# Moving a quarter of the convolution's products behind step 184 and re-pacing the convolution in a fused attention and long-convolution kernel

## The chip, the cores and the metric

The kernel runs on one core of one Trainium2 chip. The metric is the time of one execution on the device in microseconds; lower is better. A core has five engines that each run their own instruction list in order: PE (TensorE, matrix products), ACT (ScalarE, exponentials here), DVE (VectorE), POOL (GpSimd) and SP (SyncE, here only a queue that issues DMAs). They meet through semaphores.

## The reference

Two independent blocks share the launch, and their outputs are written side by side. Block A is multi-head attention with 32 heads of width 16 over 2048 tokens. Block B is a long convolution over 2048 steps for 512 channels, written with FFTs: `kv` is a 4-tap short convolution of `k` times `v`, then every channel is convolved with its own filter of length 2048, and gated by `q`.

```python
# A: x (1,2048,512), wqkv (512,1536), wo (512,512), H = 32, Dh = 16
qkv = (x @ wqkv) -> q, k, v per head
p   = softmax(q k^T * Dh**-0.5)          # 32 heads x 2048 x 2048
a   = (p v) reshaped to (1,2048,512) @ wo
# B: q, k, v (1,2048,512), shift_k (512,4), ssm_k (512,2048), ssm_D (512)
k_shift = sum_t k_pad[:, t:t+S, :] * shift_k[:, 3-t]
kv = k_shift * v
y  = irfft(rfft(kv padded to 4096) * rfft(ssm_k padded to 4096))[:, :2048]
b  = q * (y + kv * ssm_D)
out = concatenate([a, b], axis=-1)
```

## The kernel before, in words

**Attention.** The scores are cut into 2048 blocks of 128 keys by 512 queries. They are handled in 741 *steps*; a step makes the scores of two or three blocks (L539, four row groups of PE at a time), and one ACTIVATE (L550) takes the exponential of all of them from PSUM. From step 56 on, one block of a three-block step can go to DVE instead, which makes its exponential with a polynomial in five instructions: one to leave PSUM (L586), three Horner steps (L593) and a last one (L598). Two steps later the block is multiplied with the values (L632). A finished group is turned on DVE, divided by its sums, and turned back into the tile OTN (L718), whose eight slots feed the output product (L749).

**Convolution.** It is a Toeplitz product on PE. The reversed filters are written to a scratch in HBM (`kz_scratch`), and for each channel a 128 x 2048 Toeplitz tile is read back with overlapping rows: `load_wr` issues four such loads of 512 KB on SP for a *column group* `qd` of four channels. There are 128 column groups and a ring of three in SBUF (WR). `conv_lags` (L804) multiplies one group in 16 *lags* of four small products each, in column-tiled form, so there are 2048 lags in all, and they go through PSUM bank 7. The products `kv` themselves are made on PE too: a unit `("kv", c, i)` multiplies 128 channels of transposed keys (KTR) with diagonal tap matrices DG (which lie in OTN slots 4 to 7), and DVE multiplies by the values on the way out (`evac_unit`, L393). Column group `qd` needs the products of its quarter, `qd // 32`.

**The plan.** All instruction lists are written out in advance by a Python planner with its own clock: each engine has a planned time (`Eng.op`), each DMA a planned landing (`dma`, a single chain at DMA_KB kilobytes per us). In step T it emits the scores, the value products, then `emit_bg(T)`. That first lets `unit_step` place half a unit (projections of queries, keys and values, kv products, output products, and transposes of the finished convolution, "turn") if it fits before the end of the current exponential, or is forced by its due step; then it fills what is left (`room`, up to a margin) with conv lags. Until step 184 (N_EARLY) the units come from an ordered list `early`, and one PSUM bank is kept free for them throughout; after it they come from `next_unit`, by due step, in 25 slots of five steps each from step 190 on, 21 steps apart.

The lags are limited by a pace and by the planned landing of the loads:

```python
left_us = max(1.14 * (NT - END - T), 1.0)
st["lags"] = min(st["lags"] + min(PACE * st["left"] / left_us, RATE) * (pe.t - st["t"]), CAP)
left = min(LAGS, int(st["lags"]), int((room(T) - 0.06) / 0.055))
while left > 0 and ... at(h_wr[st["qd"]]) + WAIT <= pe.t:
```

and a load on the chip waits for the conv that frees its ring slot. In the kernel before, keys are loaded transposed (`load_kt`) in two slabs of 256 channels: into QN for quarters 0 and 1 and into the second half of QT for quarters 2 and 3. Both are loaded early, after the filters have been reversed on DVE (`kz_turn`). The values for quarter 2 lie in VS2, those for quarter 3 in OUTA. The weights WK (keys) and WV (values, later replaced by the output weights WO) are the halves of WKV; WK is last read by the key projection `("k", 3, 3)`.

Of the kernel before, what the change touches and what calls it, by code (L numbers as in the profile page):

```python
# [11 lines left out]
S = 2048  # L12
D = 512
H = 32
DH = 16
QB = 512
NQB = S // QB
KT = S // 128
NG = 8
# [4 lines left out]
C = 512  # L24
# [11 lines left out]
BGB = 7  # L36
N_EARLY = 184
LAGS = 6
PACE = 1.2
KEYS0 = 256  # L40
END = 16

# [20 lines left out]
GAP = 7  # L63
TAIL_GAP = 4
AHEAD = 4
KZ_LATE = 4.0
KEEP = 4
BACKLOG = 3.9
MARGIN = 0.35
SPARE = 0.1  # L70
DMA_KB = 400.0
WINDOW = 3.4
BUSY = 0.75
FILL_GAP = 0.25
RATE = 3.4
CAP = 10.0
WAIT = 1.0
LATE = 0.6
V512 = (0.60, 0.726)

# [54 lines left out]
def bass_concat_heads__mha_block__ssm_conv_h3__prompt_kernel(  # L135
# [24 lines left out]
    def sb(name, shape, dt=BF16):  # L160
# [14 lines left out]
    WQ = sb("WQ", [128, 4, D])  # L175
    PAT = sb("PAT", [1, 2, 128])
    MASK = sb("MASK", [128, 2], FP32)
    WKV = sb("WKV", [128, 2, 4, D])
    OTN = sb("OTN", [128, R_O, QB])
    DT = sb("DT", [128, QB], FP32)  # L180
    DTN = sb("DTN", [128, 2, QB])
# [8 lines left out]
    EH = sb("EH", [128, R_EH, QB], FP32)  # L190
    ZW = sb("ZW", [128, 32])
    JNK = sb("JNK", [128, 2], FP32)
    WK = WKV[:, 0, :, :]
    WV = WKV[:, 1, :, :]
    WO = WV
    VST = [x.rearrange("p (t d) -> p t d", t=NB)
           for x in (WR[:, 8, :], WR[:, 9, :], VS2[:, :], OUTA[:, :, :].rearrange("p r d -> p (r d)"))]
    KZS = WRF[:, 0:4 * LKZ].rearrange("p (c m) -> p c m", c=4)
    DSS = WRF[:, 4 * LKZ:4 * LKZ + 4].rearrange("p (c m) -> p c m", m=1)
    KTR = [QNF[:, 0:2 * LKR].rearrange("p (c s) -> p c s", c=2),  # L200
           QTF[:, NG * QB:NG * QB + 2 * LKR].rearrange("p (c s) -> p c s", c=2)]
# [54 lines left out]

    d_w = [DmaSem(sem(f"d_w{i}")) for i in range(5)]
    d_x = [DmaSem(sem(f"d_x{i}")) for i in range(4)]
    d_kv = [DmaSem(sem(f"d_kv{i}")) for i in range(6)]
# [28 lines left out]
    h_vn, h_kt, h_kt0 = [], {}, {}  # L288
    for c in range(4):
        src = bass.AP(tensor=v2.tensor, offset=v2[128 * (NB - 1), 128 * c].offset, ap=[[D, 128], [-128 * D, NB], [1, 128]])  # L290
        h_vn.append(dma(sp, d_kv[2 + c], VST[c], src, kb=1024))

    def load_kt(i, dep):
        h_kt[i] = dma(sp, d_kv[i], KTR[i][:, :, LEFT:LEFT + S], k2[:, 256 * i:256 * i + 256], [dep], transpose=True, kb=1024)
        h_kt0[i] = pool.op(lambda e: e.memset(KTR[i][:, :, 0:LEFT], 0.0), [dep])


# [19 lines left out]
    def unit_deps(u):  # L317
        if u[0] == "q":
            return h_x[u[1]] + [h_wq[min(u[2], 1)]]
        if u[0] == "k":  # L320
            return h_x[u[2]] + [h_wk[min(u[1], 1)]]
        if u[0] == "kv":
            return [h_kt[u[1] // 2], h_dg[0]]
        return h_x[u[1] // 4] + [h_wv]

    def pe_unit(u, bank, dcs=(0, 1, 2, 3)):
        kind = u[0]
        deps = [bank_free[bank]]
        mm_us, mm_run = 0.215, 0.213
        if kind == "q":  # L330
            _, qb, o = u
            deps += h_x[qb] + [h_wq[min(o, 1)]]

            def mm(e, dc):
                return e.matmul(PS[:, bank, :], lhsT=WQ[:, dc, o * 128:(o + 1) * 128], rhs=xT[:, dc, qb * 512:(qb + 1) * 512],  # L335
                                start=(dc == 0), stop=(dc == 3))
        elif kind == "k":
            _, o, sc = u
            c0 = KEYS0 if (o, sc) == (0, 0) else 0
            deps += h_x[sc] + [h_wk[min(o, 1)]]  # L340
            mm_us, mm_run = (512 - c0) / 512 * 0.215, (512 - c0) / 512 * 0.213

            def mm(e, dc):
                return e.matmul(PS[:, bank, c0:512], lhsT=WK[:, dc, o * 128:(o + 1) * 128],  # L344
                                rhs=xT[:, dc, sc * 512 + c0:(sc + 1) * 512], start=(dc == 0), stop=(dc == 3))
        elif kind == "kv":
            _, c, i = u
            deps += [h_kt[c // 2], h_kt0[c // 2], h_dg[0]]
            mm_us, mm_run = 0.27, 0.21

            def mm(e, b):
                ins = None
                for m in range(4):
                    c0 = LEFT + 128 * (4 * i + 3 - b) - m
                    ins = e.matmul(PS[:, bank, 128 * b:128 * b + 128], lhsT=KTR[c // 2][:, c % 2, c0:c0 + 128], rhs=DG[:, c, m, :],
                                   start=(m == 0), stop=(m == 3))
                return ins
        else:
            _, kt = u
            deps += h_x[kt // 4] + [h_wv]  # L360

            def mm(e, dc):
                return e.matmul(PS[:, bank, :], lhsT=xT[:, dc, kt * 128:(kt + 1) * 128], rhs=WV[:, dc, :],  # L363
                                start=(dc == 0), stop=(dc == 3))

        def fn(e):
            ins = None
            for dc in dcs:
                ins = mm(e, dc)
            return ins  # L370
        return pe.op(fn, deps, us=(0.105 + mm_us * len(dcs), 0.235 + mm_us * len(dcs)),
                     run=mm_run * len(dcs))

    def evac_unit(u, bank, h):
        kind = u[0]
        if kind == "q":
            _, qb, o = u
            for par in range(2):
                hh = h_q[(qb, 2 * o + par)] = urgent(
                    lambda e, par=par: e.tensor_scalar(QT[:, qb % 2, 2 * o + par, :], PS[:, bank, :], MASK[:, par:par + 1], None, ALU.mult),  # L380
                    [h, h_mask] + ([h_kzt[0], h_kvm[0]] if qb == 1 else []), us=V512)
        elif kind == "k":
            _, o, sc = u
            c0 = KEYS0 if (o, sc) == (0, 0) else 0
            hh = urgent(lambda e: e.tensor_copy(KTo[:, o, sc * 512 + c0:(sc + 1) * 512], PS[:, bank, c0:512]), [h],
                        us=(0.335, 0.46) if c0 else V512)
            h_k[(o, sc)] = hh
        elif kind == "kv":
            _, c, i = u
            dst = KV[:, 32 * c:32 * c + 32, NB - 4 - 4 * i:NB - 4 * i, :]  # L390
            val = VST[c][:, NB - 4 - 4 * i:NB - 4 * i, :].rearrange("p b (k c) -> p k b c", c=4)
            src = PS[:, bank, :].rearrange("p (b k c) -> p k b c", b=4, c=4)
            h_kvc[c] = hh = urgent(lambda e: e.tensor_tensor(dst, src, val, ALU.mult), [h, h_vn[c]], us=V512)  # L393
            kv_n[c] += 1
            if sum(kv_n[0:2]) == 8 and c < 2:
                load_qn(0, [h])
                wr_free.append((2, hh))
                load_wr()
            if sum(kv_n) == 16:
                h_kvm[0] = h  # L400
        else:
            _, kt = u
            dst = VAF[:, kt, 0:H * VW].rearrange("p (h e) -> p h e", e=VW)[:, :, 0:DH]
            src = PS[:, bank, :].rearrange("p (h e) -> p h e", h=H)
            hh = urgent(lambda e: e.tensor_copy(dst, src), [h, h_vaf1], us=V512)  # L405
            h_v[kt] = hh
        bank_free[bank] = hh

    h_kvc = [None] * 4
    kv_n = [0] * 4  # L410
    h_kvm = [None]
    wr_free = []
    wr_next = [0]
    h_kzw = [None]
# [274 lines left out]
    def finish_group(n, h, T):  # L689
# [21 lines left out]
        def turn_back(i0, i1, us):  # L711
# [3 lines left out]
                deps += [h_op[((p - R_O) // 4, t)] for t in range(4)]  # L715
            if p == 4:
                deps.append(h_kvm[0])
            h_otn[(p, i1)] = h_otn[p] = dve.op(lambda e: e.transpose(out=OTN[:, p % R_O, sl], in_=dtn[:, sl]), deps, us=us)  # L718

        def may_turn():  # L720
            return 2 * p in h_mul and 2 * p + 1 in h_mul and (p < R_O or all(((p - R_O) // 4, t) in h_op for t in range(4)))
        u_r, u_m, u_t = (0.155, 0.28), (0.334, 0.46), (0.6, 0.75)
        if last:
            recip(u_r)
# [39 lines left out]
    def op_out_end(qb, t, bank, h):  # L764
# [3 lines left out]
        else:  # L768
            hh = dve.op(lambda e: e.tensor_copy(dst, PS[:, bank, :]), [h])
        r0 = qb * QB + t * 128  # L770
        dma(act if t % 2 else sp, d_outE, out2[r0:r0 + 128, 0:D], dst, [hh])


    h_wr, h_qn = {}, {}
# [49 lines left out]
    def conv_turn(b, bank):  # L824
# [34 lines left out]
    state = {"qd": 0, "lag": 0, "turn": False, "q": 0, "op": 0, "started": False, "lags": 0.0,  # L859
             "left": C // 4 * NB, "t": 0.0}  # L860
# [10 lines left out]
    def next_unit(T):  # L871
# [158 lines left out]
    for T in range(NT + 3):  # L1030
# [5 lines left out]
        emit_bg(T)  # L1036
        warm_up(T)
        advance(pe.t)
    assert state["qd"] == C // 4 and not state["turn"] and state["q"] == len(later_q) and state["op"] == len(later_op), state
    assert not early_dve and not flow and not acts and not dves  # L1040


# [62 lines left out]
```

## Time and profile before

| | |
|---|---|
| median of 6 runs | 863.8 us (859.77 to 874.42) |
| the profiled execution | 859.77 us |
| its span, first to last instruction | 858.0 us |
| mean granted TensorE clock | 0.992 |
| ACT busy | 836.8 us, 98% |
| DVE busy | 782.8 us, 91% |
| PE busy (pipelined, an upper figure) | 743.3 us, 87% |
| HBM read and written | 276.83 MB, 6.42 MB |
| Toeplitz loads | 512 of 512 KB, median 8.0 us from issue to landing |
| score blocks exponentiated on DVE | 213 of 2048 |

Every time of a view below is in microseconds from the start of the span. In the view of groups and waits, "A <- B: 7.8, 20, 1.1" says that A waited for B for 7.8 us in all, 20 times, at most 1.1 us. L numbers are lines of the kernel; SPq is SP's DMA queue. In a table of windows each engine's busy time is followed by its instruction count; then come the granted PE clock (1.00 is full speed), the mean busy share of the 16 DMA engines and GB/s.

Today's places of the moved work: the sixteen kv evacuations (L393) run from 80.7 to 184.1 us, those of quarter 2 from 151.5 to 163.8 and those of quarter 3 from 169.4 to 184.1. Step 184 begins near 204 us.

### The profile page before, as it was taken

The numbers are of one execution on the slowest core, as the hardware profiler recorded it, in microseconds if no ns is written. First come the engines' busy times: TensorE is split into PE (matmuls) and PEld (weight loads), VectorE is DVE, ScalarE is ACT, GpSimd is POOL, SyncE is SP. The second block draws the span as 40 slices with busy tenths as digits, with TensorE's granted clock in tenths as the row PEclk, the third lists the DMA queues.
The fourth block names the chain that finished last, engine by engine and source line by source line (L and its number), as shares of the span: only waits on it lengthen the run. The fifth ranks groups of instructions, "written<-read, shape, count | busy, mean of one in ns | idle before, by whom it ended". The sixth has DMA issues, their size and how long they took to land.

```text
span 858.0 us, 29424 instructions
## 1 busy us (share of the span) xinstructions
PE 743.3 (87%) x13184; PEld 302.2 (35%) x13184; DVE 782.8 (91%) x1330; ACT 836.8 (98%) x746; POOL 17.3 (2%) x33
## 2 busy tenths in 40 slices
PE   7988999998888888888888888888888888888877
PEld 2223343443333333333333333333333333333332
DVE  2328999999999999999999999999999999999994
ACT  6999999999999999999999999999999999999997
POOL 2000000000000000000000000000000000000000
PEclk9999999999999999999999999999999999999999
DMA  9970069879999999999999999999999999999942
GB/s 269 258 239 1 1 207 341 279 233 328 407 407 410 361 401 396 399 407 398 387 396 373 355 392 388 407 379 394 407 408 366 408 399 410 406 394 408 407 189 74
DMA packets 104813, 289.36 MB, mean 337 GB/s; under 512 B 35184, under 2 KB 37232, under 8 KB 104304
## 3 DMA queue, kind: packets, MB, share of 16 engines
q1 hardware_dynamic: 99424, 279.35, 86.2%
q0 software_dynamic: 1808, 6.29, 2.2%
q8 instruction: 104, 1.70, 0.8%
q10 hardware_dynamic: 3456, 1.84, 0.8%
q14 instruction: 21, 0.17, 0.0%
HBM read 276.83 MB, written 6.42 MB: 330 GB/s over the span
## 4 chain that ended last, share of the span: by engine, by line
ACT 61%; DMA 16%; DVE 11%; PE 9%; SPq 2%; issue 1%; ACTq 0%
ACT PT L550 61%; DMA WR<-kz_scratch 15%; DVE EH L593 5%; PE PS L539 3%; PE PS L804 2%; DVE PTD L598 2%; SPq L223 2%; PE PS L632 2%; DVE FX L586 2%; DMA xT<-in_A_x_dram 1%; PE PS L363 1%; DVE QT L380 1%; DVE DT L696 1%; PE PS L749 0%; DVE YB L819 0%
## 5 line engine op out<-in xcount | busy, mean ns | idle before, releaser
L550 ACT ACTIVATE PT<-PS 128x1536 bf16<-128x1536 f32 (+1 forms) x741 | 833.8, 1351 | 8.7 <-PE PS L539 7.8
L539 PE MATMUL PS<-QT,KTo 32*128 32x512 bf16 x2048 | 303.2, 387 | 85.5 <-ACT PT L550 68.4
L593 DVE SCALAR_TENSOR_TENSOR EH<-EH,FX 128x512 f32<-128x512 f32 x426 | 281.9, 678 | 0.0
L804 PE MATMUL PS<-WR,KV 128*5 128x128 bf16 (+15 forms) x8192 | 223.5, 221 | 14.6 <-DMA WR<-kz_scratch 12.6
L632 PE MATMUL PS<-PT,VAF 128*32 128x512 bf16 x1835 | 201.6, 392 | 3.7 <-DVE DT L696 2.5
L804 PEld LDWEIGHTS PS<-WR,KV 128*2 128x2 bf16 (+15 forms) x8192 | 149.6, 88 | 100.6 <-issue 40.4
L539 PEld LDWEIGHTS PS<-QT,KTo 32*128 32x128 bf16 x2048 | 72.9, 91 | 263.5 <-ACT PT L550 228.1
L586 DVE TENSOR_SCALAR FX<-PS 128x512 f32<-128x512 f32 x213 | 145.2, 682 | 5.8 <-PE PS L539 5.4
L598 DVE SCALAR_TENSOR_TENSOR PTD<-EH,FX 128x512 uint16<-128x512 f32 x213 | 143.5, 676 | 0.0
L593 DVE SCALAR_TENSOR_TENSOR EH<-FX 128x512 f32<-128x512 uint16 x213 | 143.2, 680 | 0.0
L632 PEld LDWEIGHTS PS<-PT,VAF 128*32 128x32 bf16 x1835 | 48.5, 93 | 119.0 <-issue 105.8
L1012 PE MATMUL PS<-IDN,ZW 128*32 128x512 bf16 (+3 forms) x229 | 72.4, 316 | 0.0
L632 PE MATMUL PS<-PTD,VAF 128*32 128x512 bf16 x213 | 60.3, 385 | 0.0
L405 DVE CAST VAF<-PS 128x512 bf16<-128x512 f32 x16 | 11.1, 692 | 30.2 <-PE PS L363 30.2
L696 DVE STREAM_TRANSPOSE DT<-PS 128x512 f32<-128x512 f32 x31 | 22.1, 711 | 12.8 <-PE PS L632 12.2
L1012 PEld LDWEIGHTS PS<-IDN,ZW 128*32 128x32 bf16 x229 | 22.2, 97 | 11.6 <-issue 10.3
L819 DVE CAST YB<-PS 128x512 bf16<-128x512 f32 x32 | 21.8, 680 | 2.3 <-PE PS L804 2.3
L380 DVE TENSOR_SCALAR QT<-PS,MASK 128x512 bf16<-128x512 f32 x30 | 21.0, 742 | 3.0 <-PE PS L335 2.8
L363 PE MATMUL PS<-WKV,xT 128*128 128x512 bf16 x64 | 18.9, 384 | 1.8 <-DVE VAF L405 1.2
L749 PE MATMUL PS<-WKV,OTN 128*128 128x512 bf16 x64 | 19.7, 385 | 0.3 <-DVE OTN L718 0.3
L344 PE MATMUL PS<-xT,WKV 128*128 128x512 bf16 (+1 forms) x64 | 18.3, 377 | 1.1 <-DVE QT L380 0.5
L335 PE MATMUL PS<-xT,WQ 128*128 128x512 bf16 x60 | 18.2, 384 | 0.1
(66 smaller groups left out, 195.5 us busy)
## 6 DMA issues: line engine op xcount, KB each, us to landing
WR<-kz_scratch SPq DMA_DIRECT2D x512, 512.0 KB, 8.0
kz_scratch<-WR SPq DMA_DIRECT2D x1, 2176.0 KB, 8.5
QN<-in_B_q_dram POOLq DMA_DIRECT2D x2, 1024.0 KB, 12.5
out_dram<-QN POOLq DMA_DIRECT2D x2, 1024.0 KB, 8.3
out_dram<-OUTA POOLq DMA_DIRECT2D x12, 128.0 KB, 5.4
QN<-in_B_ssm_k_dram SPq DMA_DIRECT2D x1, 1024.0 KB, 6.3
QT<-in_B_ssm_k_dram SPq DMA_DIRECT2D x1, 1024.0 KB, 8.2
WR<-in_B_v_dram SPq DMA_DIRECT2D x2, 512.0 KB, 6.9
```

Source lines behind the costliest of these rows:

```text
L363: return e.matmul(PS[:, bank, :], lhsT=xT[:, dc, kt * 128:(kt + 1) * 128], rhs=WV[:, dc, :], start=(dc == 0), stop=(dc == 3))
L380: lambda e, par=par: e.tensor_scalar(QT[:, qb % 2, 2 * o + par, :], PS[:, bank, :], MASK[:, par:par + 1], None, ALU.mult),
L539: ins = e.matmul(PS[:, bank, :], lhsT=KTo[32 * s:32 * s + 32, g // 2, kt * 128:(kt + 1) * 128], rhs=QT[32 * s:32 * s + 32, qb % 2, g, :], ...
L550: h_exp[T] = act.op(lambda e: e.activation(PT[:, T % R_PT, 0:n * QB], PS[:, banks[0]:banks[0] + n, :].rearrange("p b f -> p (b f)"), ACT.E ...
L586: h_f = urgent(lambda e: e.tensor_scalar(fx, PS[:, bank, :], FIX_ADD, FIX_HI, ALU.add, ALU.min), [h, h_last.get(i - R_FX)], slack=0.6)
L593: st["h"] = dve.op(lambda e: e.scalar_tensor_tensor(eh, src, (A3, A2, A1)[j], frac, ALU.add, ALU.mult), [st["h"], h_last.get(i - R_EH), h_ ...
L598: lambda e: e.scalar_tensor_tensor(out16, eh, A4, fx, ALU.mult, ALU.add),
L632: ins = e.matmul(dst, lhsT=w, rhs=rhs, start=(k == 0), stop=(k == KT - 1), tile_position=(0, 32 * s))
L696: h_t = urgent(lambda e: e.transpose(out=dt, in_=PS[:, pvb(n), :]), [h] + before, slack=0.1, us=(0.63, 0.751))
L804: ins = e.matmul(PS[32 * c:32 * c + NB - n, BGB, 128 * (kk % 4):128 * (kk % 4) + 128], lhsT=KV[:, qd, n:NB, c], rhs=WR[:, r + c, 128 * (NB ...
L819: hh = urgent(lambda e: e.tensor_copy(YB[:, half, :].rearrange("p (k i) -> p k i", k=4), src), [h, h_yb[0]], slack=0.3, us=V512)
L1012: pe.op(lambda e: e.matmul(PS[32 * s:32 * s + 32, pvb(n), 0:128 * k], lhsT=ZW[:, :], rhs=rhs, start=False, stop=False, tile_position=(0, 3 ...
```

## The change

The kv products of quarter 3 leave the list of the early units and become jobs of `next_unit`, with due step 300. Their keys no longer come with those of quarter 2: they are loaded by themselves into the half of WKV that held WK, after the last key projection has read it. For that, WK and WV change places in WKV, which gets 16 columns more; the values of quarters 2 and 3 change places between VS2 and OUTA. The turn-back of group pair 7, which overwrites the taps of quarter 3 in OTN slot 7, waits for these products. Conv lags before step 184 fill up to 0.25 us instead of 0.35 (EARLY_MARGIN). The pace factor goes from 1.2 to 1.1; the planned load rate from 400 to 396; the guard WAIT after a planned landing from 1.0 to 1.5 us; the delay of the filter reversal after its planned landing from 4 to 8 us (KZ_LATE). At the end, the store of the second of the last four output tiles is issued by SP instead of ACT.

```diff
-PACE = 1.2
+PACE = 1.1
...
-KZ_LATE = 4.0
+KZ_LATE = 8.0
...
+EARLY_MARGIN = 0.25
+KV_DUE = 300
...
-DMA_KB = 400.0
+DMA_KB = 396
...
-WAIT = 1.0
+WAIT = 1.5
...
-    WKV = sb("WKV", [128, 2, 4, D])
+    WKV = sb("WKV", [128, 8 * D + LEFT])
...
-    WK = WKV[:, 0, :, :]
-    WV = WKV[:, 1, :, :]
+    WK = WKV[:, 4 * D:8 * D].rearrange("p (c f) -> p c f", c=4)
+    WV = WKV[:, 0:4 * D].rearrange("p (c f) -> p c f", c=4)
...
-           for x in (WR[:, 8, :], WR[:, 9, :], VS2[:, :], OUTA[:, :, :].rearrange("p r d -> p (r d)"))]
+           for x in (WR[:, 8, :], WR[:, 9, :], OUTA[:, :, :].rearrange("p r d -> p (r d)"), VS2[:, :])]
...
-           QTF[:, NG * QB:NG * QB + 2 * LKR].rearrange("p (c s) -> p c s", c=2)]
+           QTF[:, NG * QB:NG * QB + LKR].rearrange("p (c s) -> p c s", c=1),
+           WKV[:, 4 * D:4 * D + LKR].rearrange("p (c s) -> p c s", c=1)]
+    KT_OF = [(0, 0), (0, 1), (1, 0), (2, 0)]
...
     def load_kt(i, dep):
-        h_kt[i] = dma(sp, d_kv[i], KTR[i][:, :, LEFT:LEFT + S], k2[:, 256 * i:256 * i + 256], [dep], transpose=True, kb=1024)
+        h_kt[i] = dma(sp, d_kv[i], KTR[i][:, :, LEFT:LEFT + S], k2[:, (0, 256, 384)[i]:(256, 384, 512)[i]], [dep], transpose=True, kb=(1024, 512, 512)[i])
...
             h_k[(o, sc)] = hh
+            if (o, sc) == (3, 3):
+                load_kt(2, h)
...
-            if sum(kv_n) == 16:
+            if c == 2 and kv_n[c] == 4:
                 h_kvm[0] = h
+            if c == 3 and kv_n[c] == 4:
+                h_kvm[1] = h
...
             if p == 4:
                 deps.append(h_kvm[0])
+            if p == 7:
+                deps.append(h_kvm[1])
...
-            return 2 * p in h_mul and 2 * p + 1 in h_mul and (p < R_O or ...)
+            return 2 * p in h_mul and 2 * p + 1 in h_mul and (p != 7 or kv_n[3] == 4) and (p < R_O or ...)
...
-        dma(act if t % 2 else sp, d_outE, out2[r0:r0 + 128, 0:D], dst, [hh])
+        dma(act if t == 3 else sp, d_outE, out2[r0:r0 + 128, 0:D], dst, [hh])
...
-    early += [(N_EARLY - 4, ("kv", c, i)) for c in (2, 3) for i in range(4)]
+    early += [(N_EARLY - 4, ("kv", c, i)) for c in (2,) for i in range(4)]
...
     def room(T):
-        end = at(h_exp[min(T, NT - 1)]) - 0.47 - MARGIN
+        end = at(h_exp[min(T, NT - 1)]) - 0.47 - (EARLY_MARGIN if T < N_EARLY else MARGIN)
...
+        if st["kv"] < 4:
+            jobs.append((KV_DUE, ("kv", 3, st["kv"])))
         return min(jobs) if jobs else None
```

More of the change, by code (lines that the diff above doesn't have):

```diff
@@ L258, in bass_concat_heads__mha_block__ssm_conv_h3__prompt_kernel @@
     d_x = [DmaSem(sem(f"d_x{i}")) for i in range(4)]
-    d_kv = [DmaSem(sem(f"d_kv{i}")) for i in range(6)]
+    d_kv = [DmaSem(sem(f"d_kv{i}")) for i in range(7)]
     d_tap, d_kz, d_kzw, d_wo = [DmaSem(sem(n)) for n in ("d_tap", "d_kz", "d_kzw", "d_wo")]
@@ L290, in bass_concat_heads__mha_block__ssm_conv_h3__prompt_kernel @@
         src = bass.AP(tensor=v2.tensor, offset=v2[128 * (NB - 1), 128 * c].offset, ap=[[D, 128], [-128 * D, NB], [1, 128]])
-        h_vn.append(dma(sp, d_kv[2 + c], VST[c], src, kb=1024))
+        h_vn.append(dma(sp, d_kv[3 + c], VST[c], src, kb=1024))
     def load_kt(i, dep):
-        h_kt[i] = dma(sp, d_kv[i], KTR[i][:, :, LEFT:LEFT + S], k2[:, 256 * i:256 * i + 256], [dep], transpose=True, kb=1024)
+        h_kt[i] = dma(sp, d_kv[i], KTR[i][:, :, LEFT:LEFT + S], k2[:, (0, 256, 384)[i]:(256, 384, 512)[i]], [dep], transpose=True, kb=(1024, 512, 512)[i])
         h_kt0[i] = pool.op(lambda e: e.memset(KTR[i][:, :, 0:LEFT], 0.0), [dep])
@@ L322, in unit_deps @@
         if u[0] == "kv":
-            return [h_kt[u[1] // 2], h_dg[0]]
+            return [h_kt[KT_OF[u[1]][0]], h_dg[0]]
         return h_x[u[1] // 4] + [h_wv]
@@ L347, in pe_unit @@
             _, c, i = u
-            deps += [h_kt[c // 2], h_kt0[c // 2], h_dg[0]]
+            kt_i, kt_c = KT_OF[c]
+            deps += [h_kt[kt_i], h_kt0[kt_i], h_dg[0]]
             mm_us, mm_run = 0.27, 0.21
@@ L354, in mm @@
                     c0 = LEFT + 128 * (4 * i + 3 - b) - m
-                    ins = e.matmul(PS[:, bank, 128 * b:128 * b + 128], lhsT=KTR[c // 2][:, c % 2, c0:c0 + 128], rhs=DG[:, c, m, :],
+                    ins = e.matmul(PS[:, bank, 128 * b:128 * b + 128], lhsT=KTR[kt_i][:, kt_c, c0:c0 + 128], rhs=DG[:, c, m, :],
                                    start=(m == 0), stop=(m == 3))
@@ L410, in bass_concat_heads__mha_block__ssm_conv_h3__prompt_kernel @@
     kv_n = [0] * 4
-    h_kvm = [None]
+    h_kvm = [None, None]
     wr_free = []
@@ L717, in turn_back @@
                 deps.append(h_kvm[0])
+            if p == 7:
+                deps.append(h_kvm[1])
             h_otn[(p, i1)] = h_otn[p] = dve.op(lambda e: e.transpose(out=OTN[:, p % R_O, sl], in_=dtn[:, sl]), deps, us=us)
         def may_turn():
-            return 2 * p in h_mul and 2 * p + 1 in h_mul and (p < R_O or all(((p - R_O) // 4, t) in h_op for t in range(4)))
+            return 2 * p in h_mul and 2 * p + 1 in h_mul and (p != 7 or kv_n[3] == 4) and (p < R_O or all(((p - R_O) // 4, t) in h_op for t in range(4)))
         u_r, u_m, u_t = (0.155, 0.28), (0.334, 0.46), (0.6, 0.75)
@@ L855, in bass_concat_heads__mha_block__ssm_conv_h3__prompt_kernel @@
     early += [(137, ("q", 0, 3)), (138, ("k", 3, 0)), (144, ("k", 3, 1)), (150, ("k", 3, 2)), (155, ("k", 3, 3))]
-    early += [(N_EARLY - 4, ("kv", c, i)) for c in (2, 3) for i in range(4)]
+    early += [(N_EARLY - 4, ("kv", c, i)) for c in (2,) for i in range(4)]
     later_q = [("q", qb, o) for qb in range(1, NQB) for o in range(4)]
     later_op = [(qb, t) for qb in range(NQB - 1) for t in range(4)]
-    state = {"qd": 0, "lag": 0, "turn": False, "q": 0, "op": 0, "started": False, "lags": 0.0,
+    state = {"qd": 0, "lag": 0, "turn": False, "q": 0, "op": 0, "kv": 0, "started": False, "lags": 0.0,
              "left": C // 4 * NB, "t": 0.0}
     def room(T):
-        end = at(h_exp[min(T, NT - 1)]) - 0.47 - MARGIN
+        end = at(h_exp[min(T, NT - 1)]) - 0.47 - (EARLY_MARGIN if T < N_EARLY else MARGIN)
         return end - max(pe.t, at(bank_free[BGB]))
@@ L1038, in bass_concat_heads__mha_block__ssm_conv_h3__prompt_kernel @@
         advance(pe.t)
-    assert state["qd"] == C // 4 and not state["turn"] and state["q"] == len(later_q) and state["op"] == len(later_op), state
+    assert state["qd"] == C // 4 and not state["turn"] and state["q"] == len(later_q) and state["op"] == len(later_op) and state["kv"] == 4, state
     assert not early_dve and not flow and not acts and not dves
```

## The prediction

> **What bounds the kernel now.** I read the page first: shares, slices, chain.
>
> ```profile
> span 858.0 us, 29424 instructions
> ...
> PE 743.3 (87%) x13184; PEld 302.2 (35%) x13184; DVE 782.8 (91%) x1330; ACT 836.8 (98%) x746; POOL 17.3 (2%) x33
> ...
> DMA  9970069879999999999999999999999999999942
> GB/s 269 258 239 1 1 207 341 279 233 328 407 407 410 361 401 396 399 407 398 387 396 373 355 392 388 407 379 394 407 408 366 408 399 410 406 394 408 407 189 74
> ...
> ACT 61%; DMA 16%; DVE 11%; PE 9%; SPq 2%; issue 1%; ACTq 0%
> ```
>
> ACT, which makes the exponentials, is busy 98% of the span and carries 61% of the chain. But the second term of the chain is DMA, and from slice 10 on (about 215 us) the engines move around 400 GB/s without a pause: the convolution's Toeplitz loads. So there are two limits close together. Next the ACT timeline (start, length, what; idle before):
>
> ```profile
> 27.38 68.09 ACT L550 ACTIVATE PT<-PS 128x1024 bf16<-128x1024 f32 x63 [0.16 <-PE PS L539]
> 95.67 119.72 ACT L550 ACTIVATE PT<-PS 128x1024 bf16<-128x1024 f32 x116 [0.20 <-PE PS L539]
> 215.59 57.78 ACT L550 ACTIVATE PT<-PS 128x1024 bf16<-128x1024 f32 x50 [0.19 <-PE PS L539]
> 273.88 1.02 ACT L550 ACTIVATE PT<-PS 128x1024 bf16<-128x1024 f32 x1 [0.51 <-PE PS L539]
> 275.58 31.37 ACT L550 ACTIVATE PT<-PS 128x1536 bf16<-128x1536 f32 x27 [0.67 <-PE PS L539]
> ...
> 747.26 10.13 ACT L550 ACTIVATE PT<-PS 128x1536 bf16<-128x1536 f32 x9 [1.15 <-PE PS L539]
> ```
>
> Before 215 us ACT runs unbroken for 68.09 and 119.72 us; after it, it keeps running dry. How much that costs needs ACT's unbroken pace. By the groups of those stretches the first holds 39 steps of two blocks and 24 of three, the second 85 and 31. Solving 39a+24b=68.09 and 85a+31b=119.72 gives a=0.918 us and b=1.346 us. After 215.59 us:
>
> ```profile
> L550 ACT ACTIVATE PT<-PS 128x1536 bf16<-128x1536 f32 x291 | 431.1, 1564 | 4.9 <-PE PS L539 4.3
> L550 ACT ACTIVATE PT<-PS 128x1024 bf16<-128x1024 f32 x255 | 275.4, 1148 | 2.4 <-PE PS L539 2.2
> ```
>
> 291 x 1.346 + 255 x 0.918 = 625.8 us, while the last one starts at 850.43, so 634.8 us were taken: **9.0 us lost** (7.3 recorded idle; neighbouring ACTIVATEs overlap in the record, which hides the rest). Who caused it, by the waits:
>
> ```profile
> PE PS L804 <- DMA WR<-kz_scratch: 12.6, 24, 1.5
> ...
> ACT PT L550 <- PE PS L539: 7.8, 20, 1.1
> ```
>
> PE, in order, stood 12.6 us in 24 waits at the conv matmul (L804) for a load; the score matmuls (L539) for ACT queue behind it. Setting the ACT gaps beside the PE timeline: 16 gaps from 215 us on sum to 6.48 us, and 11 of them (4.96 us, 77%) come within 3.5 us of such a wait: at 214.9, 273.2, 306.3, 391.3, 407.1, 473.2, 540.4, 626.5, 744.0 and 827.9. So about 0.77 x 9.0 = 6.9 us is late loads. One more 0.75 us of the gaps (644.46, 757.68) stands in stretches of lowered clock, 12% or 1.0 us. The worst case, PE timeline and then windows (clock after the engines, then DMA share and GB/s):
>
> ```profile
> 743.95 0.52 PE L804 MATMUL PS<-WR,KV 128*16 128x128 bf16 x24 [0.84 <-DMA WR<-kz_scratch]
> ```
>
> ```profile
> 744.98:748.39 3.41, 3.41 (x57) 1.77 (x57) 1.97 (x4) 2.20 (x3) 0.00 (x0) 0.50 1.02 405
> ```
>
> PE waits 0.84 us, then has half clock for 3.41 us, and ACT loses 1.15 us. [...] The rows put a half clock right behind the waits of 273.2 and 744.0 us; I take 6.9.
>
> **How near the loads are to their limit.** Conv matmuls by window (four are one lag):
>
> ```profile
> 95.00:204.00 109.00, 22.39 (x792) 14.53 (x792) 1.00 0.70 234
> 204.00:832.00 628.00, 201.06 (x7400) 135.07 (x7400) 0.99 1.00 391
> ```
>
> Only 198 of 2048 lags are done before step 184 (204 us). A column group is 16 lags and four loads of 524,288 bytes, so a lag costs 131 KB; the other 1850 need 242 MB in 628 us, 386 GB/s, against 405 to 410 in the windows that are full. The plan wants 1.2 x 1850/(1.14 x 541) = 3.6 lags per us, capped at 3.4, or 446 GB/s: it always runs against the loads, and only its estimate of the landing plus 1.0 us guards it. That estimate is 1.280 us a load (409.6 GB/s); at 407 GB/s one takes 1.288. Over 450 loads the plan runs 3.6 us ahead of the chip, as much as it guards and more.
>
> **The change, part by part.**
>
> *Guard and rate (WAIT 1.5, DMA_KB 396).* The plan's load becomes 1.293 us (405.5 GB/s), no longer faster than the row, and 0.5 us is added to waits whose mean is 12.6/24 = 0.53. [...] The rows say 405 to 410 on this core; I use them.
>
> *PACE 1.1 and the moved products.* A kv unit is two halves of eight matmuls (0.62 us each) and a 0.68 us evacuation on DVE. Four units leave the early list: 4 x 1.29 (the plan's price) = 5.2 us of PE, which at the plan's 0.055 us a lag plus 0.06 a burst is room for about 75 lags. The smaller EARLY_MARGIN moves PE's front by 0.1 us once and adds little. With 75 more, 1775 lags are left: 370 GB/s, and a pace of 1.1 x 1775/617 = 3.16 per us, 415 GB/s, falling below 407 from about step 280. From there loads land ahead. With no extra lag the pace starts at 432 and crosses only at step 427.
>
> I let 80% of the 6.9 us go: **-5.6 us** (ends 0 and -6.9). Of the 1.0 us of clock losses without a load wait, half: **-0.5** (0 to -1.0). Next in line are transposes and slot units, the other 1.1 us, which stay.
>
> *The units after 184.* Eight halves of 0.62 us. Cover: from 240 to 300 us PE waits 5.5 us for ACT, and slots such as those at 357 and 624 us hold one unit or less. With no cover they cost 5.0 us. ACT gaps beside slot units today are about 0.3 us each: **+0.8** (0 to 5). The four DVE evacuations move with them; DVE is 98% busy on both sides, and a block on DVE is five operations of 0.68, so less than one block changes side: 0, plus or minus two blocks of 0.43 us. The POOL and DVE waits for these units (turn-back of group pair 7, near step 370) come 60 steps after their due time 300: 0.
>
> *EARLY_MARGIN.* Between 96 and 215 us ACT has no gap, but some twenty steps start right at the end of their score matmul; 20 x 0.1 = 2.0 at most, and ACT's overlap of 0.2 us or more covers most: **+0.4** (-0.2 to 2).
>
> *Loads.* The 1 MB key slab for two channel groups becomes 0.5 MB, and a second 0.5 MB transposed load is issued after the last key products (about 147 us), amid the Toeplitz loads. Nearest row: the four 512 KB transposes of x held SP 4.6 us (median) and landed in 7.8; the plan assumes 3.3. The ring holds two groups beyond the one in use, 32 lags, 17 us at the early 1.8 per us: 0 (up to +11, below). POOL's 16-column memset waits for the same product; POOL's queue has nothing due before 204 us: 0. In return the slab at 35 us holds SP about 4.8 us instead of 9.56, paying for KZ_LATE, which moves four 0.68 us copies from 21 to about 25 us. ACT gaps of 0.25 and 0.16 us lie there: 0, plus or minus 0.4. Buffer swaps and layout: same bytes, 0.
>
> *Tail.* The second of ACT's closing copies starts 0.44 us after the first, behind a 0.36 us DMA issue; that issue moves to SP, which has 0.34 us ones: **-0.4** (0 to -0.44).
>
> **Sum:** -5.6 - 0.5 + 0.8 + 0.4 - 0.4 = -5.3. The profiled execution took 859.77 us (span 858.0 and 1.8 around it), so its like would take 854.5. It is the lowest of six, 4.0 below their median 863.8. If late loads are what varies, the slower runs gain more; I keep half of the 4.0: **856.5 us**, 0.85% under the median. About 0.5% (4.3 us) is what this measurement can tell from no change.
>
> **Rivals.**
>
> *Loads stay late (860 to 865, say 863; 0.19).* The 628 us window averages 391 GB/s, below the plan's 405.5, and the median run may be below the profiled one. Then a new guard only delays the conv, catching up brings the waits back, and the +0.8 and +0.4 eat the rest. Against: windows with a full queue show 405 to 410.
>
> *It does not do what it says (about 859.5; 0.10).* Before step 176 the planner offers later units once the early list is empty. The q units of block 1 already run at 186 to 195 us that way. With four kv units fewer on the list, these q units move up and kv fits behind them before 184. The early conv gains nothing, the loads stay at 95%, and only the guard works: about half of 5.6. Half of this case lies beyond 0.5%.
>
> *The mid-stream transpose starves the conv (slower: 866 to 871; 0.14).* Place: 147 to 165 us. If SP is held as by the 1 MB slab (9.56 us issue, 13.1 to landing) and the loads behind it outlast the ring's 17 us (less the 8.0 us that a load itself takes), PE stands up to 8 us at L804, ACT with it, and two or three half-clock windows add 3: 859.8 - 5.3 + 11 = 865.5, plus up to 4 for the median. It decides from about 10 us of lost loading. Against: half the bytes, and DMA only 70% busy there.
>
> **Numbers.** Forecast 0.57 (853 to 859.4). Faster 0.57 + 0.04 = 0.61, same 0.19 + 0.06 = 0.25, slower 0.14. Range 852 to 865.5: it takes in the first two rivals, leaves out the third and a little below.
>
> **What would show it.** Right: L804's waits for WR under 4 us in all, ACT unbroken for 100 us and more after 280, three half-clock spells fewer, more than 250 lags before step 184, DMA below 1.00 in the last third. Wrong: PE waiting for WR near 150 to 165 us; kv evacuations all before 204 us; ACT gaps in the slots of steps 190 to 260; or the 12.6 us still there.

## The result, and the profile after

The changed kernel takes 859.11 us (median of 33 executions, 853.73 to 864.47) against 863.3 us before (70 executions): 0.9962 of it, 95% interval 0.9947 to 0.9977. A second measurement beside a variant (after2, below) gave 0.9925 (0.9899 to 0.995). It is faster, by 0.4 to 0.75%; 856.5 us had been forecast, 0.85% under the 863.8 us then known. Ratios leave out the few executions more than 1.5% above the fastest of their kernel, which show a lower clock too (0.969 to 0.978 in the experiments' runs of the kernel before); medians are of all.

The profiled execution of the first measurement, 864.75 us with a mean clock of 0.981, is the slowest of its kernel; the one before, 859.77 us, was the fastest of six. The page of the changed kernel:

```profile
PE 749.3 (87%) x13177; PEld 303.5 (35%) x13177; DVE 785.3 (91%) x1335; ACT 836.5 (97%) x746; POOL 17.4 (2%) x34
...
PEclk9999999999979999999999988999999999999999
...
ACT 75%; PE 9%; DMA 7%; DVE 7%; SPq 1%; issue 1%
```

ACT's work is the same to 0.3 us, and DMA's share of the chain has fallen from 16% to 7%. In its place the clock row, all nines before, shows a 7 and two 8s. The waits of this execution, and then of the profiled execution of after2 (858.0 us, near its kernel's median):

```profile
ACT PT L559 <- PE PS L548: 13.7, 29, 1.4
...
PE PS L815 <- DMA WR<-kz_scratch: 5.2, 7, 1.2
```

```profile
ACT PT L559 <- PE PS L548: 7.6, 15, 1.1
PE PS L815 <- DMA WR<-kz_scratch: 5.2, 10, 1.3
```

The conv (now L815) waits for loads 5.2 us instead of 12.6, in both. But ACT's waits for PE, 7.8 us before, have not fallen with them: 13.7 us in the first of these executions, 7.6 in the second. The ACT timeline of the first:

```profile
95.53 117.65 ACT L559 ACTIVATE PT<-PS 128x1024 bf16<-128x1024 f32 x114 [0.31 <-PE PS L548]
214.00 25.18 ACT L559 ACTIVATE PT<-PS 128x1024 bf16<-128x1024 f32 x22 [0.82 <-PE PS L548]
239.57 1.45 ACT L559 ACTIVATE PT<-PS 128x1536 bf16<-128x1536 f32 x1 [0.39 <-PE PS L548]
241.84 1.02 ACT L559 ACTIVATE PT<-PS 128x1024 bf16<-128x1024 f32 x1 [0.82 <-PE PS L548]
...
557.86 129.90 ACT L559 ACTIVATE PT<-PS 128x1536 bf16<-128x1536 f32 x114 [0.48 <-PE PS L548]
```

ACT still runs dry, now in clusters from about 239, 336 and 510 us. The first one by windows (PE, PEld, DVE, ACT, POOL, clock, DMA):

```profile
233.09:236.50 3.41, 2.11 (x26) 0.66 (x25) 3.41 (x7) 3.41 (x4) 0.00 (x0) 1.00 1.03 406
236.50:246.74 10.24, 10.05 (x115) 3.04 (x116) 7.79 (x14) 7.81 (x8) 0.00 (x0) 0.50 0.65 251
```

No load is late here: PE is merely short of work for 3.41 us (busy 62%; the plan has no conv lag in two steps of it), then has half clock for 10.24 us, in which ACT stands 2.4 us. In after2 ACT stands 2.4 us too, in five gaps from 237.3 to 245.1 us, at a mean clock of 0.96 from 204 to 290 us. The kv evacuations of quarter 3 (tile VS), which were to come after step 184 (near 204 us), come out here:

```profile
L400 DVE TENSOR_TENSOR KV<-PS,VS x4: 677/679/691, 186.7 to 216.6; 128x512 bf16<-128x512 f32 x4
```

By the PE timeline three of the four units run in steps 162 to 175 and only the fourth in steps 193 and 194. The early conv:

```profile
95.00:204.00 109.00, 25.25 (x936) 16.46 (x928) 1.00 0.83 282
```

936/4 = 234 lags instead of 198.

### The profile page after: what moved, and what is told of

It is laid out like the page before. It is cut to its first block, busy times and chain, and to the rows that moved or that the text cites. A ratio compares the mean times of both kernels' runs of the same rounds, so it can differ in the third digit from the quotient of the medians.

```text
span 863.0 us, 29400 instructions
## 1 busy us (share of the span) xinstructions
PE 749.3 (87%) x13177; PEld 303.5 (35%) x13177; DVE 785.3 (91%) x1335; ACT 836.5 (97%) x746; POOL 17.4 (2%) x34
## 4 chain that ended last, share of the span: by engine, by line
ACT 75%; PE 9%; DMA 7%; DVE 7%; SPq 1%; issue 1%
ACT PT L559 74%; DMA WR<-kz_scratch 7%; PE PS L548 3%; DVE EH L602 3%; PE PS L641 2%; PE PS L815 2%; DVE FX L595 1%; DVE PTD L607 1%; SPq L227 1%; PE PS L760 1%; DMA xT<-in_A_x_dram 1%; PE PS L368 1%; DVE QT L385 0%; DVE VAF L414 0%; DVE DT L705 0%
## 5 line engine op out<-in xcount | busy, mean ns | idle before, releaser
L559 ACT ACTIVATE PT<-PS 128x1536 bf16<-128x1536 f32 (+1 forms) x741 | 833.6, 1373 | 14.1 <-PE PS L548 13.7
L548 PE MATMUL PS<-QT,KTo 32*128 32x512 bf16 x2048 | 308.3, 389 | 91.8 <-ACT PT L559 76.7
L815 PE MATMUL PS<-WR,KV 128*14 128x128 bf16 (+15 forms) x8192 | 221.3, 222 | 6.1 <-DMA WR<-kz_scratch 5.2
L815 PEld LDWEIGHTS PS<-WR,KV 128*8 128x8 bf16 (+15 forms) x8192 | 151.1, 88 | 88.9 <-issue 44.5
L1025 PE MATMUL PS<-IDN,ZW 128*32 128x512 bf16 (+3 forms) x222 | 71.9, 324 | 0.0
L1025 PEld LDWEIGHTS PS<-IDN,ZW 128*32 128x32 bf16 x222 | 21.4, 96 | 11.2 <-issue 10.5
```

The lines of the kernel that those rows point to most:

```text
L548: ins = e.matmul(PS[:, bank, :], lhsT=KTo[32 * s:32 * s + 32, g // 2, kt * 128:(kt + 1) * 128], rhs=QT[32 * s:32 * s + 32, qb % 2, g, :], ...
L559: h_exp[T] = act.op(lambda e: e.activation(PT[:, T % R_PT, 0:n * QB], PS[:, banks[0]:banks[0] + n, :].rearrange("p b f -> p (b f)"), ACT.E ...
L815: ins = e.matmul(PS[32 * c:32 * c + NB - n, BGB, 128 * (kk % 4):128 * (kk % 4) + 128], lhsT=KV[:, qd, n:NB, c], rhs=WR[:, r + c, 128 * (NB ...
L1025: pe.op(lambda e: e.matmul(PS[32 * s:32 * s + 32, pvb(n), 0:128 * k], lhsT=ZW[:, :], rhs=rhs, start=False, stop=False, tile_position=(0, 3 ...
```

## What varies between executions

Every execution comes with its mean clock. Over the 35 executions of the changed kernel on record, time follows 1334.8 - 479.7 x clock, with a correlation of -0.90; over 123 of the kernel before, taken in four sessions with the experiments, 1440.0 - 583.3 x clock, correlation -0.91. One half-clock window of 3.413 us lowers the clock of an execution by 0.5 x 3.413/858 = 0.0020, so by these slopes it goes with about 1 us. The mean clock was 0.9879 before and is 0.9905 after. Carried on to full clock the two lines stand at 856.7 and 855.1 us. So, as an estimate, of 4 us gained some 1.6 (0.5 to 2.7, by resampling the executions) are fewer stalls at full clock, and the rest is clock: about 7.1 us (0.0121 x 583) went with it before, and about 4.6 us (0.0095 x 480) still do. The correlation alone does not say what lowers the clock in a longer execution; the experiments below bear on that.

## Experiments

Medians and ratios to the kernel before, with the number of executions and their mean clock. Medians of different sessions are up to 2.5 us apart for the kernel before (862.3 to 864.8), so compare ratios:

| kernel | median us | ratio, 95% interval | executions | mean clock |
|---|---|---|---|---|
| b_guard | 862.46 | 1.0006 (0.9983 to 1.0029) | 12 | 0.986 |
| a_noguard | 862.97 | 1.0006 (0.9981 to 1.003) | 22 | 0.987 |
| a_kvearly | 862.63 | 0.9984 (0.9952 to 1.0015) | 14 | 0.986 |
| a_kvlate | 854.03 | 0.988 (0.9843 to 0.9917) | 6 | 0.996 |
| after2 | 857.65 | 0.9925 (0.9899 to 0.995) | 6 | 0.9945 |
| kvlate2 | 853.88 | 0.9889 (0.986 to 0.9919) | 6 | 0.9955 |
| l_noguard | 873.25 | 1.0096 (1.0062 to 1.013) | 6 | 0.982 |
| a_cold | 880.15 | 1.0171 (1.0109 to 1.0232) | 4 | 0.940 |
| b_fill | 858.48 | 0.9938 (0.9917 to 0.9959) | 15 | 0.996 |
| a_fill | 863.75 | 1.0001 (0.9978 to 1.0024) | 22 | 0.988 |
| a_kb | 864.2 | 0.9994 (0.9959 to 1.003) | 12 | 0.984 |
| a_fill_kb | 858.3 | 0.9946 (0.992 to 0.9972) | 12 | 0.995 |
| b_fill_kb | 860.47 | 0.9977 (0.9953 to 1.0001) | 12 | 0.994 |
| a_fill_kb_w1 | 858.68 | 0.9956 (0.9927 to 0.9986) | 12 | 0.993 |
| a_fill_share_w1 | 855.4 | 0.9894 (0.9857 to 0.993) | 6 | 0.9975 |
| l_kb | 854.92 | 0.9905 (0.9875 to 0.9936) | 6 | 0.993 |

**Is it the guard?** Alone on the kernel before, and taken out of the changed one (the edit below, reversed):

```diff
-DMA_KB = 400.0
+DMA_KB = 396
-WAIT = 1.0
+WAIT = 1.5
```

> The kernel before with the guard alone (WAIT 1.5, DMA_KB 396). Theory G: undoing the guard in the changed kernel took all of its gain, so the guard alone should bring most of it: waits of the conv for loads under 8 us, 859.5 to 861.5 us, ratio to before 0.9955 to 0.998. Rival (the guard only pays with the earlier lags and the slower pace, since the loads are at 95% of their limit): waits under 8 us all the same, but the conv runs up to the last steps and loses there or in emptier PE windows (mean clock at or under 0.988): 862 to 864.

> The changed kernel with the guard undone (WAIT 1.0, DMA_KB 400). Theory G (the guard is what gave the gain): the conv's waits for loads go from 5 back to 9 us or more and the time to 861.5 to 864. Rival (pace and the earlier lags gave it): the waits stay under 7 us and the time at 858 to 860.5.

Waits of b_guard:

```profile
ACT PT L550 <- PE PS L539: 11.1, 23, 1.3
...
PE PS L804 <- DMA WR<-kz_scratch: 6.3, 9, 1.9
```

The rival held for b_guard: the load waits are halved, as the prediction's step had it, and nothing is gained. ACT waits longer for PE than before (7.8). Near 318.5 and 420.9 us three score matmuls go from 0.39 us to 0.58 and 0.47, and ahead of both places no conv matmul waits; PE waits for ACT, 0.63 us just before, with nothing else planned. Its PE timeline:

```profile
317.06 0.39 PE L539 MATMUL PS<-QT,KTo 32*128 32x512 bf16 x3 [0.88 <-ACT PT L550]
...
318.40 0.58 PE L539 MATMUL PS<-QT,KTo 32*128 32x512 bf16 x3 [0.63 <-ACT PT L550]
```

The second of these is already slowed (0.58 us instead of 0.39; at half clock in the kernel before, at 274.92 us, three took 0.61). Without the guard the changed kernel's gain is gone (8.3 us of load waits in its profile). So the guard is needed, but by itself it swaps one stall for another.

**Is it the moved work?** The four units put back into the early list (a_kvearly), and the four held back until step 184 (a_kvlate). The edit of the second:

```diff
-        if st["kv"] < 4:
+        if st["kv"] < 4 and T >= N_EARLY:
```

> The changed kernel with the four products of quarter 3 put back into the early list (keys still loaded into the key-weight half, all constants as changed). Theory S: the plan makes three of the four units before step 184 in the changed kernel too, so putting them back costs 20 early lags of 235 and nothing else: 858 to 860.5 us. Rival (the move carries the gain): waits for loads rise above 8 us and the time to 861 to 863.

> The changed kernel, with the products of quarter 3 kept back until step 184 for all four units (in the changed kernel the plan makes three of them before). Theory S: where they are made matters little in itself; query units take the free places, early lags fall from 235 to 222, loads wait a little more: 859.5 to 862. Rival (the change gives more where it does what it says): more early conv and fewer waits, 856 to 858.

> The changed kernel itself once more, beside a_kvlate on one chip. By its 33 executions: 858 to 860.5 us, mean clock 0.989 to 0.992.

> a_kvlate once more (all four units of quarter 3 after step 184). Theory M (the move was not made, and making it gives the missing gain: units fill PE's empty windows from 204 to 290 us, query units go before): 853 to 856 us, 3 us or more under after2, mean clock 0.994 or more. Rival (chance): within 1.5 us of after2.

This is the line the change lacks. `next_unit` offers later units as soon as the early list is empty, and without this condition it offers the kv units too, from about step 152. With it the kernel gains 1.1 to 1.2% over the kernel before, in two measurements; beside the changed kernel itself 853.88 against 857.65 us (after2, a little under its own expectation). The theory I had held for a_kvlate, that the place matters little, was wrong, and the rival's 856 to 858 was still too high; theory M of kvlate2 held. Where it comes from shows in one window, first after2, then kvlate2:

```profile
204.00:290.00 86.00, 71.82 (x1365) 29.98 (x1364) 81.83 (x139) 82.90 (x74) 1.32 (x2) 0.96 0.97 373
```

```profile
204.00:290.00 86.00, 74.24 (x1559) 33.53 (x1546) 85.49 (x147) 86.00 (x77) 0.77 (x1) 1.00 1.02 393
```

With the units in this stage (evacuated from 216.8 to 287.6 us) PE has more to do (busy 74.24 us instead of 71.82), its clock is 1.00 instead of 0.96, the DMA engines are busy without a pause (1.02, 393 GB/s), and ACT is busy for the whole 86.00 us instead of 82.90: 3.1 us, of 3.8 between the medians. The other two profiles agree: 86.00 us in a_kvlate, 82.72 in the first profile of the changed kernel. The early stage loses little: 886 conv matmuls to 204 us instead of 940 (852 in a_kvlate). The ACT timeline of kvlate2 is what the prediction had wanted to see:

```profile
186.52 172.82 ACT L559 ACTIVATE PT<-PS 128x1536 bf16<-128x1536 f32 x153 [0.42 <-PE PS L548]
359.51 215.50 ACT L559 ACTIVATE PT<-PS 128x1536 bf16<-128x1536 f32 x188 [0.18 <-PE PS L548]
```

Holding the kv units back also lets four more query units run before step 184; whether those or the kv units themselves matter was not separated. a_kvearly ended at the time of its rival, but not by its waits (5.6 us for loads, where over 8 were expected). It lies between the changed kernel and the one before, and its interval takes in both.

The guard undone under the moved units:

> a_kvlate with the guard undone (WAIT 1.0, DMA_KB 400). Theory G: the guard is worth 4 us here as it was without the move: 857 to 861, waits for loads 9 us or more. Rival (the move alone carries it): 853 to 856.5.

```profile
151.01 0.30 PE L815 MATMUL PS<-WR,KV 128*16 128x128 bf16 x8 [2.20 <-DMA WR<-kz_scratch]
```

```profile
L227 SPq DMA_TRANSPOSE WKV<-in_B_k_dram x1: 3836/3836/3836, 158.1 to 158.1; - x1
```

It ends at 873.25 us, 19 above kvlate2, with load waits of 19.0 us; far more than expected. (The planner lays this variant out anew, so a part of the 19 us can be its order.) Its longest wait, the first line, ended before the transposed key slab was issued at 158.1 us, so that slab did not cause it. POOL's 1 MB load of QN was issued at 137.6 us; whether it delayed the load waited for was not tested.

**Is it the clock?** Every keep-warm product left out of the changed kernel after step 3. (These are the matmuls of L1025 that add zero: the planner puts them where PE would otherwise have nothing to do.)

```diff
-BUSY = 0.75
+BUSY = 0.0
```

> The changed kernel without any keep-warm product after step 3 (222 of them left out; they add zero). Theory C: PE's clock, not the loads, carries what is left; windows of PE with little work become many, the mean clock falls to 0.95 or below and the time rises by about 480 to 800 us per unit of clock, to 880 us or more. If keep-warm products matter little, the clock stays over 0.985 and the time under 865.

```profile
ACT PT L559 <- PE PS L548: 24.0, 49, 1.3
...
PE PS L815 <- DMA WR<-kz_scratch: 1.2, 3, 0.5
```

21 us slower, with 1.2 us of load waits left. Its four executions run from 0.959 to 0.927 in clock and lie on a slope of 442 us per unit. So here PE, with less to do, ran at a mean clock of 0.940 instead of 0.9905 and lost time with it, without late loads. The opposite, larger keep-warm products (up to three matmuls in a row):

```diff
-BUSY = 0.75
+BUSY = 0.95
...
-        k = min(int(gap / 0.055), int((BUSY * WINDOW - lately) / 0.054) + 1, 4)
+        k = min(int(gap / 0.055), int((BUSY * WINDOW - lately) / 0.054) + 1, 12)
```

> The kernel before, with the same larger keep-warm products. Theory C2: in the kernel before the half-clock spells follow waits for loads, and PE, in order, can't run dummies while a conv matmul stands at its head: 861 to 863 us, clock up by at most 0.003, waits of the conv for loads still 10 us or more. Rival: it loses its clock in empty steps just as the changed kernel does; then it gains as much as that one, 2 us or more, and ends at 859 to 861.

> The changed kernel, with the keep-warm products (L1025) allowed to be up to three matmuls of 512 columns instead of one where PE has nothing else to do (and the limit on lately used PE time at 0.95 instead of 0.75). Theory C (clock): what the changed kernel still loses is half-clock spells that begin where PE has run out of planned work. Over its 35 runs time goes as 1334.8 - 479.7 x mean clock; filling the idle time brings the clock from about 0.991 to 0.996 or more, so 855 to 857.5 us, 0.990 to 0.9935 of before. Theory L (loads): what is left is conv waits for loads, which dummy products can't shorten; then the clock stays at or under 0.992 and the time at 858 to 860.

Both expectations failed. The kernel before gains 0.6% by it alone, about as much as by the whole change, though its load waits stay (15.7 us in 28); its mean clock goes from 0.988 to 0.996, so there too empty steps had cost clock. The changed kernel gains nothing and loses against itself. In its profile (869.98 us, one of its slowest, at a mean clock of 0.982) PE stood in load waits up to 2.1 us:

```profile
ACT PT L559 <- PE PS L548: 17.5, 28, 2.1
...
PE PS L815 <- DMA WR<-kz_scratch: 6.0, 6, 2.1
```

One of these waits, of 1.85 us, ends at 494.99 us, where the gate tile QN is stored and reloaded. The plan counts each of these 1 MB transfers at 512 KB. Corrected:

```diff
-    ... d_q[0], QN[:, :, :], q2[...], deps)
+    ... d_q[0], QN[:, :, :], q2[...], deps, kb=1024)
-    ho = dma(pool, d_outB[0], dst, QN[:, :, :], [hh])
+    ho = dma(pool, d_outB[0], dst, QN[:, :, :], [hh], kb=1024)
```

> The changed kernel with the larger keep-warm products and with the two 1 MB transfers of the gate tile QN (its store near 484 us and reload near 495 us) counted by the plan at 1 MB instead of 512 KB. Theory K: the larger keep-warm products lost because PE then stood in deeper load waits (2.06, 1.85, 1.36 us), some of them behind transfers that the plan counts too small; with the right size the wait near 495 us is under 1 us, the mean clock over 0.991 and the time 858 to 861. Rival I (the loads are late because POOL's transfers share the DMA engines with loads already queued, whatever size the plan gives them): the wait near 495 us stays over 1 us and the time at 862 to 865.

> The changed kernel with only the right size (1 MB) of the two QN transfers in the plan; keep-warm products as in the changed kernel. Two factors stand between a_fill (863.8 us) and a_fill_kb (858.3). Theory K1: right sizes without larger keep-warm products save the deep wait near 495 us but leave the empty PE windows: mean clock 0.989 to 0.992, 858.5 to 860.5 us. Rival K2 (the sizes alone do it): mean clock 0.994 or more, 857 to 858.5.

> The kernel before with the larger keep-warm products and the right size of the two QN transfers in the plan. b_fill took 858.5 us at a mean clock of 0.996. Theory K: a little better, 857 to 858.5. Rival I: no change, 858 to 859.5.

With both edits the changed kernel comes to 858.3, in its range; with the size alone to 864.2, nearly 4 us over the expectation. The kernel before with both takes 860.5, over both its ranges: the size adds nothing to the larger products there. So neither edit helps the changed kernel alone, and together they bring it back to about where it stood without either, in this order of the plan. The profile of a_fill_kb, its fastest execution (853.22 us), has a mean clock of 1.000, and ACT waits 4.9 us. A general effect of the size can't be read from these three. With PE kept warm, the guard WAIT lowered to 1.0 us, and then a plan that lets POOL's transfers push back the loads in flight:

> a_fill_kb with the guard WAIT back at 1.0 us (DMA_KB stays 396). With PE kept warm the guard's own worth shows. Theory G: the conv's waits for loads rise from 3.7 us to 7 or more, the deepest empty a window of PE and halve its clock, mean clock 0.991 or less, 860 to 863 us. Rival W (the guard is worth little where the clock is kept): mean clock 0.994 or more, 857 to 859.

> a_fill_kb_w1 (WAIT 1.0), but the plan moves every load still in flight back by the time of a transfer that POOL issues, instead of queueing that transfer behind them. Theory I (the late loads are those that POOL's transfers overtake): waits over 1 us are gone, waits in all under 5 us although the guard is small, mean clock 0.994 or more, 856.5 to 858.5 us. If lateness comes from elsewhere, it ends where a_fill_kb_w1 does, within 1 us.

Load waits go back up to 12.2 us in 20 waits, and the time stays at 858.7, at a mean clock of 0.993 (0.995 in a_fill_kb): beside the larger products this half of the guard is worth little (DMA_KB stays at 396, which l_noguard undid too). Pushing the loads back gives 855.4 on the same chip, 3.3 us less. Waits were still 9.1 us, at most 1.5, so they did not vanish as expected; the time fell all the same, with the highest mean clock of all, 0.9975. Why is not shown.

**The best version.** The moved units with the right size:

> a_kvlate with the right size (1 MB) of the two QN transfers in the plan. Theory: the move keeps the clock, the size saves the wait near 495 us: 852 to 855. Rival (right sizes do not help by themselves, as a_kb did not: 864): 855 to 859.

854.92 us, inside its range, but not under kvlate2. The fastest version is a_kvlate: 854.0 and 853.9 us, 1.1 to 1.2% under the kernel before.

PACE, EARLY_MARGIN and KZ_LATE were not varied by themselves, so how the changed kernel's own gain divides between them, the guard and the one moved unit stays open.

## Why the prediction was wrong, point by point

**Part that failed first: the moved products.** "Four units leave the early list ... room for about 75 lags." Only one left the early stage, and the whole change brought 36 more early lags. I had read in the code that this could happen and gave it 0.10, at 859.5 us; measured 859.1. The first half of that rival is what happened: three units ran before step 184. Its number is partly luck, since it has the early conv gain nothing and the guard work for half of 5.6 us, while the early conv did gain and the guard alone brought nothing (b_guard). It could have been settled by following `next_unit` from step 152 on: nothing in it holds a job with due step 300 back. With the units held back the kernel beats the forecast (853.9 us), but not by this step: the early lags are then 221 (886/4), fewer than in the changed kernel, while four more query units run before step 184. The gain lies in the stage after 204 us.

**The guard, -5.6 us.** The load waits fell nearly as forecast (12.6 to 5.2 us; under 4 was wanted). The step that failed is that their removal is a gain in time. b_guard shows 6.3 us fewer waits for nothing: PE, held back by plan, was as empty there as where it had waited at its head (busy 1.90 of the 3.41 us before 318.5 us; in the kernel before, 1.95 of those before 273.94, with a load wait of 1.46 in them), and it was slowed the same (0.58 us for three score matmuls, there 0.61).

**The clock, -0.5 us, and "half of the 4.0 us".** I took the half clock as a follower of load waits and hence the spread of executions as late loads. The spread goes with the clock: correlation -0.9 in both kernels, and a mean that the change lifts by 0.0026 only, 1.3 windows of 3.413 us in an execution. "Three half-clock spells fewer" did not come: the first profile has four before the tail, as before, and longer ones; after2, with a clock of 0.96 from 204 to 290 us, 0.99 from there to 420 and 1.00 to 835, has by these about three windows of half clock, against four before. The term was mis-sized: about 4.6 us remain there. And b_fill has a mean clock of 0.996 with 15.7 us of load waits in its profile, so late loads alone did not lower it there.

**My reading of the half clock** was too narrow. In 233.09 to 236.50 us PE was busy 62%, without a load wait, and three windows at half clock (10.24 us) followed; I had the clock fall after load waits only.

**The units after 184, +0.8.** In the changed kernel one unit ran there (PE, 214.8 to 216.6 us), and no ACT gap stands beside it; the 0.82 us gap at 214.00 comes just before, behind a load wait of 1.16 us. With all four there (kvlate2) the stage 204 to 290 us has no ACT gap at all; the term should have been zero or negative.

**The tail, -0.4.** ACT's closing copies, 1.03 us apart before, run back to back, as forecast. But SP now has a third store to issue, at 860.4 us, and that is the last one. First before, then after:

```profile
854.13 0.60 ACT L767 ACTIVATE QT<-PS 128x512 bf16<-128x512 f32 x1 [2.99 <-PE PS L749]
...
855.79 0.36 ACTq L223 DMA_DIRECT2D out_dram<-QT  x1
```

```profile
859.04 1.09 ACT L778 ACTIVATE QT<-PS 128x512 bf16<-128x512 f32 x2 [2.99 <-PE PS L760]
...
L227 SPq DMA_DIRECT2D out_dram<-QT x3: 337/431/453, 859.5 to 860.4; - x3
```

From the start of the first copy to the end of the span it is 3.87 us before (858.0 - 854.13) and 3.96 after (863.0 - 859.04; 3.94 in after2 and kvlate2). The tail gained nothing.

**Right:** EARLY_MARGIN and KZ_LATE cost nothing. From 95.53 us ACT runs unbroken for 117.65 us over 84 steps of two blocks and 30 of three, which at the prediction's pace take 117.5; the early gaps of 0.25 and 0.16 us are unchanged. The loads do hold 399 to 414 GB/s in full windows.

**The mid-stream transpose** did not starve the conv: no wait there in the changed kernel, and, as shown above, the wait at 151.01 us in l_noguard is not its doing. But I had mis-sized the load:

```profile
L227 SPq DMA_TRANSPOSE WKV<-in_B_k_dram x1: 7524/7524/7524, 152.7 to 152.7; - x1
```

512 KB held SP for 7.5 us, not 4.6, and the slab at 35 us for 7.6, not 4.8.

## What to carry to other kernels

Where a static plan fills one engine beside another that is the bound, look at the clock of every execution before explaining their spread, and check windows for PE work, not for PE waits: here the guard alone turned half of the waits into planned pauses (12.6 to 6.3 us) and gained nothing (1.0006), where the pauses were as empty. When a diff says that work moves past a point, follow the planner's conditions to see what keeps it from running earlier. Moved work is not only a cost at its new place: in kvlate2 PE's clock was 1.00 from 204 to 290 us, and 0.96 in after2, where three of the four units ran before it.

## What the runs showed of the hardware

In the profiles of the first measurement, before and after, the half-clock spells start on a grid of 3.413 us, fixed within each profile, and those that end before the tail end on it. From 20 to 845 us I took every window of this grid that stood at full clock, its PE busy share as the profile shows it, and the clock of the window after it. No share was under 0.55. From 0.55 to 0.65, 4 of 5 windows were followed by half clock; from 0.65 to 0.76, 4 of 50; above, 0 of 414. The eight that were followed by half clock, first before, then after (PE, PEld, DVE, ACT, POOL, clock, DMA):

```profile
270.53:273.94 3.41, 1.95 (x66) 0.91 (x54) 2.44 (x5) 2.90 (x4) 0.00 (x0) 1.00 1.02 405
639.17:642.58 3.41, 2.51 (x51) 0.84 (x38) 3.41 (x7) 3.41 (x4) 0.00 (x0) 1.00 1.03 410
741.57:744.98 3.41, 2.31 (x39) 0.79 (x37) 3.41 (x6) 3.41 (x3) 0.00 (x0) 1.00 1.01 405
751.81:755.22 3.41, 2.35 (x40) 0.85 (x28) 3.41 (x7) 3.41 (x5) 0.00 (x0) 1.00 1.01 399
```

```profile
233.09:236.50 3.41, 2.11 (x26) 0.66 (x25) 3.41 (x7) 3.41 (x4) 0.00 (x0) 1.00 1.03 406
332.07:335.48 3.41, 2.00 (x33) 0.67 (x29) 3.41 (x7) 3.41 (x4) 0.00 (x0) 1.00 1.04 410
506.15:509.56 3.41, 2.58 (x43) 0.81 (x35) 3.31 (x6) 3.41 (x4) 0.00 (x0) 1.00 1.03 408
550.53:553.94 3.41, 2.03 (x16) 0.50 (x15) 3.41 (x7) 3.41 (x4) 0.00 (x0) 1.00 1.01 414
```

So in these two executions the clock goes with how much PE did in one window, but not by the share alone: after 816.76 to 820.17 us in the changed kernel, with PE busy 2.18 of 3.41 us, it stayed full.

The time that a transposed load held SP did not follow its bytes: in the changed kernel the slab of 2048 rows and 256 columns (1 MB) held it for 6.3 us at the start, while the two of 128 columns (512 KB) held it for 7.6 and 7.5. It is no constant of the slab either: the last of these took 3.8 us in l_noguard, issued 5 us later. What sets it was not separated.
